# Attention and gated feed-forward on one core: a new order of scores and value products in the second half of the first batch

## The chip, the core and the metric

The kernel runs on one core of one Trainium2 chip. The metric is device time in microseconds for one launch, lower is better. A core has TensorE (matrix products, which write into PSUM), VectorE, ScalarE and GpSimd (elementwise work), and SyncE, which here only issues DMAs. GpSimd issues DMAs too. Each engine works through its own queue of instructions in order and waits at an instruction until the semaphores that it names have arrived. PSUM has eight banks of 128 x 512 fp32 here.

## The reference

Two steps follow each other, on 4 batches of 768 tokens with 8 heads of 64.

First an attention in which a query sees the first 8 keys (the globals) and the last 96 keys up to itself, with a bias that falls with the distance:

```
scores = q @ k.T / sqrt(64) - slope[h] * dist        # dist = 96 for globals out of the window
scores = where(is_global | is_local, scores, -1e9)
attn   = softmax(scores) @ v                          # (4, 8, 768, 64)
```

Then, with the heads of a token side by side as x (3072 x 512), a gated feed-forward:

```
out = (maximum(x @ w_gate, 0) * (x @ w_val)) @ w_out  # w_gate, w_val: 512 x 1536; w_out: 1536 x 512
```

## The kernel before, in words

**Tiling.** The work is cut into eight halves of 384 tokens, two to a batch; a half is called s in the attention and chunk c in the feed-forward. Heads go in pairs p = 0 to 3. Keys are cut into seven tiles j of 120 keys with the 8 globals in front of each. Chunk c needs the attention of half s = c, of all four pairs, as the bf16 tile xT.

**Attention of the first two halves (s = 0, 1).** For a pair p the pieces are:

- C(p), `piece_cast` (line 240): the fp32 q and k of the pair are cast to bf16, two instructions, on an engine chosen by s and p. In half 1 before the change: pair 0 GpSimd, 1 ScalarE, 2 VectorE, 3 GpSimd.
- T(p), `piece_t`: TensorE transposes them into one av bank, and four VectorE copies bring them to qT and kT.
- BI(p, g) and SC(p, g): the keys' tiles are in two groups g. The bias of a group is written into a score tile of two PSUM banks, the scores are added to it, and ScalarE's Exp (line 356) makes the bf16 tile es. Two such score tiles are in turn in half 1.
- AW(p), `piece_av_wide` (line 417): ten products with a matrix of ones give the softmax sums, ten with v the values (line 431). ScalarE takes Ln of the sums (line 437) and Exp of its negative (line 439), and VectorE multiplies the values with it into xT (line 442). Sums and values are two tiles of the av pool (two banks), except in half 0 for odd p, where they are the two banks of one score tile.

**Feed-forward.** `ffn_pieces` (line 477) gives for each of 12 blocks fc a gate tile (line 485, four products, then a relu on ScalarE, line 488) and a value tile (line 495, four products, then VectorE's multiply with the relu, line 497), and then the output products (line 504). Until the end of half 1 gate and value tiles share two PSUM banks; later they have three.

**Order.** It is written out by hand: pieces are called one after the other, and each engine's queue has its instructions in the order of these calls. `attention_pieces` (line 445) returns the list of a half; for half 1 its argument `fill` has six feed-forward pieces of chunk 0 which stand between the attention's pieces: value tiles 2 and 3, gate tiles 4, 5 and 6, value tile 4. Ahead of the list gates 0 to 3 and value tiles 0 and 1 are called, after it value tiles 5 and 6, gate 7, value tile 7; then chunk 1 begins. Which bank of a pool a tile gets is decided when the program is built: the one that is planned to be free first. So two tiles that are taken one after the other can lie in one bank.

**GpSimd's queue.** After half 0's list it holds the cast of pair 0 of half 1 (`piece_cast(1, 0)`), the loads of v for half 1, and the loads of weight group 1 (`load_w_group(1)`: gate and value weights of blocks 4 to 7, lines 168 to 176), then casts from half 1's list, then group 2 and the memsets that let SyncE's loads of q and k of half 2 begin.

Of the kernel before, what the change touches and what calls it, by code (L numbers as in the profile page):

```python
# [10 lines left out]
AF = mybir.ActivationFunctionType  # L11
# [4 lines left out]
def kernel(  # L16
# [12 lines left out]
    nc = tc.nc  # L29
# [9 lines left out]
    QH = S // 2  # L39
# [6 lines left out]
    scale = 1.0 / math.sqrt(D)  # L46
# [63 lines left out]
    GW = 4  # L110
# [29 lines left out]
    def load_v_globals(b):  # L140
        nc.gpsimd.dma_start(out=v_dst(b, 0, NG, 0),
                            in_=v[b, :, 0:NG, :].rearrange("h p d -> p h d"))

    def spread_v_globals(b, j0=1, j1=NT):
        for j in range(j0, j1):
            nc.sync.dma_start(out=v_dst(b, 0, NG, j), in_=v_dst(b, 0, NG, 0))
# [16 lines left out]
    def load_v_half(s):  # L163
        b, half = divmod(s, 2)
        if half == 0 and s > 2:
            load_v_globals(b)
            spread_v_globals(b)
        for j in range(4) if half == 0 else range(4, NT):
            load_v(b, j)

    def load_w(dst, src, f0, f1):
        nc.gpsimd.dma_start(out=dst, in_=src[:, f0:f1].rearrange("(c p) f -> p c f", p=128))

    def load_w_group(i):
        load_w(wg[i], moe_w_gate, i * GW * 128, (i + 1) * GW * 128)
        load_w(wv[i], moe_w_val, i * GW * 128, (i + 1) * GW * 128)
# [64 lines left out]
    def piece_cast(s, p):  # L241
        qk = cast_pool.tile([128, 2, NN, 2, D], BF16, name="qk")
        cast_of[s, p] = qk
        for i, src in ((1, ks_of[s]), (0, qs_of[s])):
            copy = nc.gpsimd.tensor_copy
            if s == 0:
                copy = (nc.vector.tensor_copy, nc.scalar.copy, nc.scalar.copy, nc.vector.tensor_copy)[p]
            elif s == 1 and p in (1, 2):
                copy = (nc.scalar.copy, nc.vector.tensor_copy)[p - 1]
            copy(  # L250
                qk[:, i].rearrange("t n e d -> t e n d"),
                src[:, 2 * p : 2 * p + 2, :].rearrange("t e (n d) -> t e n d", n=NN))
# [164 lines left out]
    def piece_av_wide(s, p):  # L417

        todo = [t for group in first_groups[s] for t in group]
        if s == 0 and p % 2 == 1:  # L420
            t = P["qk"].tile([128, 2, 512], FP32, name="qk_ps")
            av = [t[:, i] for i in range(2)]
        else:
            av = [av_psum.tile([128, 512], FP32, name="av_ps") for _ in range(2)]
        for what in range(2):
            av3 = av[what][:, 0:QH].rearrange("d (n p) -> d n p", n=NN)
            for i, (j, a, w, m) in enumerate(todo):
                es, c = es_of[s, p, j]
                for e in range(2):
                    z0 = D + 2 * D * (2 * p + e)  # L430
                    nc.tensor.matmul(av3[64 * e : 64 * e + 64, :, a : a + w],  # L431
                                     lhsT=ones if what == 0 else vbuf[0][:, j, z0 : z0 + D],
                                     rhs=es[:, e, c : c + NN * w].rearrange("k (n p) -> k n p", n=NN),
                                     start=(i == 0), stop=(i == len(todo) - 1),
                                     skip_group_check=True)
        ln = rc_pool.tile([128, QH], FP32, name="lnd")
        nc.scalar.activation(ln, av[0][:, 0:QH], AF.Ln, bias=0.0, scale=1.0)
        rc = rc_pool.tile([128, QH], FP32, name="rcp")
        nc.scalar.activation(rc, ln, AF.Exp, bias=0.0, scale=-1.0)
        if s not in xT_of:  # L440
            xT_of[s] = xt_pool.tile([128, N_DC, QH], BF16, name="xT")
        nc.vector.tensor_tensor(xT_of[s][:, p, :], av[1][:, 0:QH], rc, op=ALU.mult)

    def attention_pieces(s, fill=()):
        T = lambda p: [(0.34, lambda: piece_t(s, p))]
        QK = lambda p: [(0.18, lambda g=g: piece_qk(s, p, g)) for g in range(3)]
        AW = lambda p: [(0.58, lambda: piece_av_wide(s, p))]
        C = lambda p: [(0.0, lambda: piece_cast(s, p))]
        BI = lambda p, *gs: [(0.2, lambda g=g: piece_bias(s, p, g)) for g in gs]
        SC = lambda p, *gs: [(0.2, lambda g=g: piece_score(s, p, g)) for g in gs]  # L450
        X = lambda *fs: [(0.0, f) for f in fs]
        if s == 0:
            return (C(0) + X(lambda: load_v_globals(0), lambda: load_v(0, 0), lambda: load_v(0, 1),
                             lambda: load_v(0, 2), lambda: load_v(0, 3), lambda: load_w_group(0))
                    + C(1) + T(0) + BI(0, 0, 1) + C(2) + T(1) + SC(0, 0, 1) + BI(1, 0) + SC(1, 0) + C(3) + T(2)
                    + BI(1, 1) + SC(1, 1) + BI(2, 0) + T(3) + X(lambda: copy_v_globals(0, 1, 4))
                    + SC(2, 0) + BI(2, 1) + SC(2, 1)
                    + BI(3, 0) + SC(3, 0) + BI(3, 1) + SC(3, 1)
                    + AW(0) + AW(1) + X(lambda: load_qk_after(1, nc.vector, True)) + AW(2)
                    + AW(3) + X(second_pools, lambda: warm(4)))  # L460
        if s == 1:
            f = [[x] for x in fill]
            return (C(1) + T(0) + BI(0, 0, 1) + T(1) + C(2) + SC(0, 0, 1) + f[0] + BI(1, 0) + SC(1, 0)
                    + BI(1, 1) + SC(1, 1) + C(3) + T(2) + f[1] + BI(2, 0) + SC(2, 0) + BI(2, 1) + T(3)
                    + AW(0) + SC(2, 1) + BI(3, 0) + SC(3, 0) + f[2] + AW(1)
                    + BI(3, 1) + SC(3, 1) + f[3] + AW(2) + f[4] + f[5] + AW(3))
        AV = lambda p: [(0.29, lambda e=e: piece_av(s, p, e)) for e in range(2)]
        g = QK(3)
        a = AV(2)
        return (QK(0) + QK(1) + AV(0) + QK(2) + AV(1) + g[0:1] + a[0:1] + g[1:2] + a[1:2] + g[2:3]  # L470
                + [(0.0, lambda: None)] * 2 + AV(3))
# [2 lines left out]

    out_v = out.rearrange("(s p n) d -> s n p d", p=128, n=NN)

    def ffn_pieces(c):
        ht = ht_pool.tile([128, N_FC, QH], BF16, name="ht")
        st = {}

        def gate(fc):
            xT = xT_of[c]
            psg = P["ff"].tile([128, 512], FP32, name="ff_ps")
            for dc in range(N_DC):
                nc.tensor.matmul(psg[:, 0:QH], lhsT=w_of(wg, dc, fc), rhs=xT[:, dc, :],  # L485
                                 start=(dc == 0), stop=(dc == N_DC - 1))
            gr = gr_pool.tile([128, QH], BF16, name="grelu")
            nc.scalar.activation(gr, psg[:, 0:QH], AF.Relu, bias=0.0, scale=1.0)  # L488
            st[fc] = gr

        def val(fc):
            xT = xT_of[c]
            psv = P["ff"].tile([128, 512], FP32, name="ff_ps")
            for dc in range(N_DC):
                nc.tensor.matmul(psv[:, 0:QH], lhsT=w_of(wv, dc, fc), rhs=xT[:, dc, :],  # L495
                                 start=(dc == 0), stop=(dc == N_DC - 1))
            nc.vector.tensor_tensor(ht[:, fc, :], psv[:, 0:QH], st[fc], op=ALU.mult)  # L497

        def outp(n, part):
            if part == 0:  # L500
                st["o"] = P["ff"].tile([128, 512], FP32, name="ff_ps")
            ps2 = st["o"]
            for fc in range(part * N_FC // 2, (part + 1) * N_FC // 2):
                nc.tensor.matmul(ps2, lhsT=ht[:, fc, n * 128 : (n + 1) * 128],  # L504
                                 rhs=wo_sb[:, fc, :],
                                 start=(fc == 0), stop=(fc == N_FC - 1))
            if part == 1:
                osb = osb_pool.tile([128, DM], FP32, name="osb")
                nc.scalar.copy(osb, ps2)  # L509
                nc.sync.dma_start(out=out_v[c, n], in_=osb)  # L510

        f1 = []
        for fc in range(N_FC):
            f1.append((0.65, lambda fc=fc: gate(fc)))
            f1.append((0.65, lambda fc=fc: val(fc)))
        f2 = []
        for n in range(NN):
            for part in range(2):
                f2.append((1.3, lambda n=n, part=part: outp(n, part)))
        return f1, f2  # L520
# [26 lines left out]
        nc.gpsimd.memset(kT[0][p][:, 6, NG + 48 : 128].bitcast(mybir.dt.uint32), 0)  # L547
    piece_cast(1, 0)
    load_v_half(1)
    load_w_group(1)  # L550

    f1_0, f2_0 = ffn_pieces(0)
    f1_1, f2_1 = ffn_pieces(1)
    G = [slice(2 * GW * i, 2 * GW * (i + 1)) for i in range(N_FC // GW)]
    for i in (0, 2, 4, 6, 1, 3):
# [19 lines left out]
    for p in range(HP):  # L575
        piece_cast(2, p)
# [59 lines left out]
```

## Time and profile before

| | |
|---|---|
| median of 4 runs | 254.96 us (253.32 to 255.2) |
| the profiled execution's own time | 253.32 us |
| its span in the profile | 251.2 us |
| TensorE busy in the span | 241.0 us (96%) |
| ScalarE, VectorE, GpSimd busy | 158.3, 132.5, 88.6 us |
| granted TensorE clock, mean | 0.998 |

The profile is of one execution. "Busy" is the time in which an engine had an instruction at work; TensorE's products overlap, so the length of one row and the distance to the next row's start differ, and distances between starts are what adds up. In a row of the order in time the first number is the start in microseconds from the start of the span, the second the length of the merged group, and brackets hold the idle time ahead of it and what ended that. In a row of a stretch each engine has its busy time and its count.

### The profile page before, as it was taken

The numbers are of one execution on the slowest core, as the hardware profiler recorded it, in microseconds if no ns is written. First come the engines' busy times: TensorE is split into PE (matmuls) and PEld (weight loads), VectorE is DVE, ScalarE is ACT, GpSimd is POOL, SyncE is SP. The second block draws the span as 40 slices with busy tenths as digits, with TensorE's granted clock in tenths as the row PEclk, the third lists the DMA queues.
The fourth block names the chain that finished last, engine by engine and source line by source line (L and its number), as shares of the span: only waits on it lengthen the run. The fifth ranks groups of instructions, "written<-read, shape, count | busy, mean of one in ns | idle before, by whom it ended". The sixth has DMA issues, their size and how long they took to land.

```text
span 251.2 us, 4902 instructions
## 1 busy us (share of the span) xinstructions
PE 241.0 (96%) x1751; PEld 142.6 (57%) x1751; DVE 132.5 (53%) x338; ACT 158.3 (63%) x319; POOL 88.6 (35%) x211
## 2 busy tenths in 40 slices
PE   7789999999999999999999999999999999999993
PEld 3556665666555666556655666556555666556541
DVE  4745634875464657427662567437662557424410
ACT  5886785637675787557774787557774687553321
POOL 7907995500557327503626075303610000000000
PEclk9999999999999999999999999999999999999999
DMA  6999999981899995938469958838432100030012
GB/s 174 161 191 255 160 229 239 190 134 49 251 139 258 179 214 129 121 108 248 109 83 92 271 145 147 76 102 247 109 83 83 43 3 1 16 112 0 0 42 83
DMA packets 77559, 33.13 MB, mean 132 GB/s; under 512 B 53472, under 2 KB 74464, under 8 KB 77536
## 3 DMA queue, kind: packets, MB, share of 16 engines
q1 hardware_dynamic: 45680, 24.93, 37.2%
q0 software_dynamic: 31856, 7.91, 32.2%
q8 instruction: 13, 0.21, 0.4%
q14 instruction: 10, 0.08, 0.1%
HBM read 28.38 MB, written 6.29 MB: 138 GB/s over the span
## 4 chain that ended last, share of the span: by engine, by line
PE 82%; DVE 4%; ACT 4%; POOL 3%; DMA 3%; issue 1%; POOLq 0%; ACTq 0%; DVEq 0%
PE ff_ps L504 25%; PE ff_ps L485 22%; PE ff_ps L495 22%; PE av_ps L397 5%; PE qk_ps L369 4%; DMA wg<-in_moe_w_gate_dram 3%; DVE xT L414 2%; DVE ht L497 2%; POOL vbuf L155 1%; PE av_ps L281 1%; PE qk_ps L334 1%; PE av_ps L431 1%; ACT rcp L411 1%; ACT lnd L406 1%; ACT grelu L488 1%
## 5 line engine op out<-in xcount | busy, mean ns | idle before, releaser
L495 PE MATMUL ff_ps<-xT,wv 128*128 128x384 bf16 x384 | 77.8, 326 | 1.2 <-DVE ht L497 0.7
L485 PE MATMUL ff_ps<-xT,wg 128*128 128x384 bf16 x384 | 77.9, 326 | 0.6 <-DVE ht L497 0.5
L488 ACT ACTIVATE grelu<-ff_ps 128x384 bf16<-128x384 f32 x96 | 47.0, 489 | 33.1 <-PE ff_ps L485 16.9
L504 PE MATMUL ff_ps<-wo_sb,ht 128*128 128x512 bf16 x288 | 67.1, 379 | 0.0
L497 DVE TENSOR_TENSOR ht<-ff_ps,grelu 128x384 bf16<-128x384 f32 x96 | 53.4, 558 | 24.5 <-PE ff_ps L495 20.4
L414 DVE TENSOR_TENSOR xT<-av_ps,rcp 64x384 bf16<-64x384 f32 x48 | 26.6, 555 | 45.6 <-ACT rcp L411 42.7
L485 PEld LDWEIGHTS <-wg 128*128 128x128 bf16 x384 | 36.1, 97 | 24.5 <-issue 1.2
L495 PEld LDWEIGHTS <-wv 128*128 128x128 bf16 x384 | 36.1, 97 | 23.6 <-issue 2.7
L381 DVE TENSOR_TENSOR es<-es,m_all 128x432 bf16<-128x432 bf16 (+5 forms) x108 | 33.2, 335 | 22.4 <-ACT es L372 21.9
L372 ACT ACTIVATE es<-qk_ps 128x432 bf16<-128x432 f32 (+2 forms) x72 | 37.8, 528 | 10.3 <-PE qk_ps L369 8.4
L504 PEld LDWEIGHTS <-ht 128*128 128x128 bf16 x288 | 27.0, 97 | 28.2
L294 POOL CAST kc<-ks 128x384 bf16<-128x384 f32 x20 | 9.8, 533 | 59.1 <-DMA ks<-in_k_dram 59.1
L406 ACT ACTIVATE lnd<-av_ps 64x384 f32<-64x384 f32 x48 | 23.3, 485 | 11.7 <-PE av_ps L397 11.0
L509 ACT COPY osb<-ff_ps 128x512 f32<-128x512 f32 x24 | 14.0, 585 | 25.4 <-PE ff_ps L504 24.6
L369 PE MATMUL qk_ps<-qT,kT 128*128 128x432 bf16 (+5 forms) x108 | 24.8, 286 | 0.0
L155 POOL DMA_DIRECT2D vbuf<-in_v_dram x28 | 24.3, 878 | 0.6 <-issue 0.6
L397 PEld LDWEIGHTS <-vbuf 128*128 128x128 bf16 x216 | 18.0, 98 | 7.4
L397 PE MATMUL av_ps<-es,vbuf 128*128 128x216 bf16 (+4 forms) x216 | 21.0, 226 | 0.0
L369 PEld LDWEIGHTS <-kT 128*128 128x128 bf16 x108 | 10.6, 98 | 7.6
L302 POOL CAST qz<-qs 128x192 bf16<-128x192 f32 x40 | 12.6, 362 | 3.6 <-DMA qs<-in_q_dram 3.1
L411 ACT ACTIVATE rcp<-lnd 128x384 f32<-128x384 f32 x24 | 12.5, 522 | 0.8
L356 ACT ACTIVATE es<-qk_ps 128x864 bf16<-128x864 f32 (+3 forms) x16 | 10.6, 707 | 3.3 <-PE qk_ps L351 3.2
(77 smaller groups left out, 143.4 us busy)
## 6 DMA issues: line engine op xcount, KB each, us to landing
out_dram<-osb SPq DMA_DIRECT2D x24, 256.0 KB
ks<-in_k_dram SPq DMA_DIRECT2D x5, 768.0 KB
qs<-in_q_dram SPq DMA_DIRECT2D x5, 768.0 KB
vbuf<-in_v_dram POOLq DMA_DIRECT2D x24, 120.0 KB, 4.7
ks<-in_k_dram SPq DMA_DIRECT2D x12, 192.0 KB
qs<-in_q_dram SPq DMA_DIRECT2D x12, 192.0 KB
wg<-in_moe_w_gate_dram POOLq DMA_DIRECT2D x3, 512.0 KB, 7.7
wv<-in_moe_w_val_dram POOLq DMA_DIRECT2D x3, 512.0 KB, 9.5
```

Of the source, the lines that this page charges most:

```text
L155: nc.gpsimd.dma_start(out=v_dst(b, NG + r0, NG + r0 + n, j), in_=v[b, :, KT * j + r0 : KT * j + r0 + n, :].rearrange("h p d -> p h d"))
L369: nc.tensor.matmul(ps[:, c : c + n_], lhsT=kt[:, j, :], rhs=qd[:, :, :, a : a + w], start=True, stop=True)
L372: nc.scalar.activation(es[:, 0:cols], ps[:, 0:cols], AF.Exp, bias=0.0, scale=scale)
L381: nc.vector.tensor_mul(e4, e4, mk)
L397: nc.tensor.matmul(av3[:, :, a : a + w], lhsT=vb[:, j, z0 : z0 + 128], rhs=es[:, c : c + NN * w].rearrange("k (n p) -> k n p", n=NN), star ...
L406: nc.scalar.activation(ln[o0 : o0 + 64], av[d0 : d0 + 64, 0:QH], AF.Ln, bias=0.0, scale=1.0)
L414: nc.vector.tensor_tensor(xT_of[s][r, p, :], av_of[s, p, e_][r, 0:QH], rc[r], op=ALU.mult)
L485: nc.tensor.matmul(psg[:, 0:QH], lhsT=w_of(wg, dc, fc), rhs=xT[:, dc, :], start=(dc == 0), stop=(dc == N_DC - 1))
L488: nc.scalar.activation(gr, psg[:, 0:QH], AF.Relu, bias=0.0, scale=1.0)
L495: nc.tensor.matmul(psv[:, 0:QH], lhsT=w_of(wv, dc, fc), rhs=xT[:, dc, :], start=(dc == 0), stop=(dc == N_DC - 1))
L497: nc.vector.tensor_tensor(ht[:, fc, :], psv[:, 0:QH], st[fc], op=ALU.mult)
L504: nc.tensor.matmul(ps2, lhsT=ht[:, fc, n * 128 : (n + 1) * 128], rhs=wo_sb[:, fc, :], start=(fc == 0), stop=(fc == N_FC - 1))
```

## The change

Four things change, all of them in half 1 and chunk 0:

- the order of half 1's list: all bias and score pieces come ahead of the four value products; the fill pieces stand at other places, and pair 3's cast and transpose come earlier;
- value products of odd p take their two tiles from the score pool in half 1 too, as in half 0;
- the relus of gates 4, 5 and 6 of chunk 0 are VectorE instructions;
- of half 1's casts, pair 3 is VectorE's and pair 2 GpSimd's, and the latter is called ahead of the loads of weight group 1.

```diff
@@ piece_cast
-            elif s == 1 and p in (1, 2):
-                copy = (nc.scalar.copy, nc.vector.tensor_copy)[p - 1]
+            elif s == 1 and p % 2 == 1:
+                copy = (nc.scalar.copy, nc.vector.tensor_copy)[p // 2]
@@ piece_av_wide
-        if s == 0 and p % 2 == 1:
+        if p % 2 == 1:
@@ attention_pieces
-            return (C(1) + T(0) + BI(0, 0, 1) + T(1) + C(2) + SC(0, 0, 1) + f[0] + BI(1, 0) + SC(1, 0)
-                    + BI(1, 1) + SC(1, 1) + C(3) + T(2) + f[1] + BI(2, 0) + SC(2, 0) + BI(2, 1) + T(3)
-                    + AW(0) + SC(2, 1) + BI(3, 0) + SC(3, 0) + f[2] + AW(1)
-                    + BI(3, 1) + SC(3, 1) + f[3] + AW(2) + f[4] + f[5] + AW(3))
+            return (C(1) + T(0) + BI(0, 0, 1) + T(1) + SC(0, 0, 1) + f[0] + C(3) + BI(1, 0) + SC(1, 0)
+                    + BI(1, 1) + SC(1, 1) + T(2) + f[1] + BI(2, 0) + SC(2, 0) + T(3) + BI(2, 1) + SC(2, 1)
+                    + BI(3, 0) + SC(3, 0) + BI(3, 1) + SC(3, 1) + AW(0) + AW(1) + f[2] + AW(2) + f[3]
+                    + AW(3) + f[4] + f[5])
@@ ffn_pieces
-    def ffn_pieces(c):
+    def ffn_pieces(c, by_vector=()):
...
-            nc.scalar.activation(gr, psg[:, 0:QH], AF.Relu, bias=0.0, scale=1.0)
+            if fc in by_vector:
+                nc.vector.tensor_scalar_max(gr, psg[:, 0:QH], 0.0)
+            else:
+                nc.scalar.activation(gr, psg[:, 0:QH], AF.Relu, bias=0.0, scale=1.0)
@@ after half 0
     piece_cast(1, 0)
     load_v_half(1)
+    piece_cast(1, 2)
     load_w_group(1)
-    f1_0, f2_0 = ffn_pieces(0)
+    f1_0, f2_0 = ffn_pieces(0, range(GW, 2 * GW - 1))
```

## The prediction

> **What bounds the kernel now.** I read the stretches first, cut where the kernel's stages change, then TensorE's own waits in the stretch that the diff touches, then TensorE in order of time there.
>
> Stretches (the columns are busy time and count of TensorE, its weight loads, VectorE, ScalarE, GpSimd, then granted clock, DMA share, GB/s):
>
> ```profile
> 0.00:17.40 17.40, 13.49 (x163) 8.21 (x163) 8.92 (x33) 13.31 (x29) 10.84 (x25) 1.00 1.13 169
> 17.40:40.00 22.60, 21.46 (x250) 14.04 (x251) 12.19 (x31) 14.48 (x27) 18.48 (x40) 1.00 1.20 218
> 40.00:240.00 200.00, 198.81 (x1308) 117.29 (x1307) 111.28 (x274) 128.77 (x261) 59.27 (x147) 1.00 0.63 122
> ```
>
> From 40 us to the end TensorE is 99.4% busy at full clock, in an order that the diff doesn't change. So a microsecond won or lost before 40 us arrives at the end one for one, and nothing else counts. The change works between 17.4 and 40 us, where TensorE idles for 22.60 - 21.46 = 1.14 us. That is already close to the ceiling of any gain: 0.45% of the time.
>
> TensorE's waits from 17 to 40 us, then its order there (start, length, what, and in brackets the idle time and its releaser):
>
> ```profile
> PE av_ps L431 <- ACT lnd L437: 0.6, 1, 0.6
> PE ff_ps L485 <- DVE ht L497: 0.5, 1, 0.5
> PE ff_ps L485 <- DMA wg<-in_moe_w_gate_dram: 0.2, 1, 0.2
> ```
>
> ```profile
> 24.57 0.51 PE L334 MATMUL qk_ps<-dd,sid 128*128 128x216 bf16 x4
> ...
> 28.31 0.49 PE L431 MATMUL av_ps<-es,ones 128*64 128x216 bf16 x10
> 29.39 0.49 PE L431 MATMUL av_ps<-es,vbuf 128*64 128x216 bf16 x10 [0.58 <-ACT lnd L437]
> ...
> 35.76 0.49 PE L431 MATMUL av_ps<-es,ones 128*64 128x216 bf16 x10
> 36.10 0.47 PE L431 MATMUL av_ps<-es,vbuf 128*64 128x216 bf16 x10
> 36.50 1.48 PE L495 MATMUL ff_ps<-xT,wv 128*128 128x384 bf16 x8
> 38.45 0.81 PE L485 MATMUL ff_ps<-xT,wg 128*128 128x384 bf16 x4 [0.47 <-DVE ht L497]
> ```
>
> Two stalls. At 28.31 the first value product (pair 0) puts its sums into an av bank; its value half waits until ScalarE's Ln has read those sums, because the pool gave both tiles the same bank. At 38.45 gate 7 waits for a feed-forward bank that VectorE frees late, since the last xT multiply (37.38) stands ahead of it in VectorE's queue.
>
> **A sum to compare with.** From the starts in that order I take, per piece: transpose 0.34, first bias group 0.45, its scores 0.28, second bias group 0.36, its scores 0.23, one gate or value tile 0.65 (26.23 to 26.88), a whole value product 0.74 (33.62 to 34.36). From 24.57 (first bias of pair 1) to the first gate of chunk 1 stand: bias and scores of three pairs 3 x 1.32 = 3.96, two transposes 0.68, four value products 2.96, nine feed-forward tiles 5.85, together 13.45. A piece followed by a value product takes 0.1 longer (0.75 instead of 0.65 at 30.78, 32.87, 35.02; 0.43 instead of 0.34 at 27.88): four times, 0.40. Idle, start to start: 29.39 - 28.31 - 0.33 = 0.75, and 38.45 - 36.50 - 1.30 = 0.65. Sum 24.57 + 13.45 + 0.40 + 1.40 = 39.82; the trace has that gate at 39.75. So the sum is good to 0.1 us.
>
> **The change, part by part.**
>
> *Pools and order.* All products keep their number and shape, so 13.45 stays. With scores ahead, pair 0's product comes after pair 3's scores. In the built program its sums and values then lie in two av banks, pairs 1 and 3 use the score banks, pair 2 the av banks again. The 0.75 goes. Value products are entered after another kind of piece three times instead of four: 0.30, so -0.10. What is late next: the score groups now run without value products between them, and two score tiles go round. Pair 3's first bias needs the bank of pair 2's first scores. On my clock those scores start at 27.33, their Exp at 27.72 (as in the trace) and it lasts 0.85, to 28.57; TensorE reaches the bias at 28.54 (27.61 + transpose 0.34 + 0.36 + 0.23) and starts at 28.62, as the trace starts a bias 0.05 after the Exp it waits for. Cost 0.08. Pair 3's scores need the copies of its transpose, done on VectorE near 29.1, when they begin: nothing. Pair 2's product (32.3) needs pair 0's Ln and xT: ScalarE does the eight Exps to 30.87, then Ln, Exp of pair 0 to 31.8, xT to 32.4; the sums half hides it. If ScalarE were 0.3 us later, that would show.
>
> *Casts.* Pair 3's cast goes to VectorE, pair 2's to GpSimd. VectorE first has value tile 2's multiply (24.56 to 25.03), then the casts at the trace's spacing (0.75 each) to 26.53, so pair 2's transpose copies start 0.10 later than at 26.43; the scores that need the third copy have 0.10 to spare: nothing. Pair 2 on GpSimd is ready at 25.1 where its transpose starts at 25.89. The price is in GpSimd's queue:
>
> ```profile
> 23.48 0.65 POOL L155 DMA_DIRECT2D vbuf<-in_v_dram  x1
> 24.11 0.79 POOL L172 DMA_DIRECT2D wg<-in_moe_w_gate_dram  x1
> 24.88 0.77 POOL L172 DMA_DIRECT2D wv<-in_moe_w_val_dram  x1
> 25.62 0.56 POOL L250 CAST qk<-ks 128x384 bf16<-128x384 f32 x1
> 26.13 0.49 POOL L250 CAST qk<-qs 128x384 bf16<-128x384 f32 x1
> 26.58 0.75 POOL L172 DMA_DIRECT2D wg<-in_moe_w_gate_dram  x1
> ```
>
> The two casts move ahead of the loads of weight group 1: issue at 25.07 instead of 24.11; what follows them (group 2 at 26.58, then the memsets that release SyncE's q and k loads) keeps its time. Group 1's gate weights landed 6.5 us after issue, at 30.6, and gate 4 ran at 30.78: no slack in the old order. In the new one gate 4 stands behind two value products: scores end at 29.95, +0.10, + 2 x 0.74 = 31.53. A full shift gives 31.57, a wait of 0.04. I expect less: the packets under 512 B, which are those of v, run until 27.75 on the same queue, past the new issue's end (25.9), so the slowest DMA engines reach the weights no later. Bounds of the landing: 30.6 to 31.6; I take no wait. The value weights of group 1 (8.9 us, at most 34.8) meet value tile 4 at 35.1: hidden by 0.3.
>
> Here a rule speaks against the change. The Trainium skill, "SBUF — State Buffer", § Who interferes with whom, says that a VectorE copy or cast in its two-port modes and GpSimd take one port pair in turns and the second is blocked for the whole instruction, descriptor writing included. The new VectorE casts (25.03 to 26.6) lie upon the issue of group 1. But so do the old ones:
>
> ```profile
> 24.25 0.84 DVE L250 CAST qk<-ks 128x384 bf16<-128x384 f32 x1
> 25.00 0.82 DVE L250 CAST qk<-qs 128x384 bf16<-128x384 f32 x1
> ```
>
> Early in the kernel such a cast takes 0.36; here it is VectorE that loses, and the issue beside it takes 0.79 against 0.75 for group 2, beside which VectorE casts nothing. By the rule, with GpSimd the loser, two casts of 0.36 to 0.42 add up to 0.8 to the issue: landing 32.4 at worst, gate 4 waits 0.9, and the end is 255.3. By the row it is 0.04. I take the row.
>
> *Relus on VectorE.* Relus 4 to 6 leave ScalarE (0.49 each), which waits for nothing of importance by then. The trace has no VectorE relu; bounds for 384 columns out of PSUM are 0.35 (bf16 copy) and 0.56 (the multiply, fp32), and I take the multiply's row, next start after 0.47, since its PSUM input is fp32. Their place matters more: VectorE's queue becomes xT0, xT1, relu 4, xT2, relu 5, xT3, relu 6, then the multiplies. Let pair 3's product start at x. Today xT3 starts at x + 1.62 and the next VectorE instruction at x + 2.09. In the new order that is relu 6, done at x + 2.6; value tile 5 needs its bank, is wanted at x + 0.74 + 2 x 0.65 = x + 2.04 and starts at x + 2.65: a wait of 0.61. So the second stall isn't removed, it moves to another tile with nearly the same length. Gate 7 then needs the bank of value tile 5: a bank is free 1.53 after its tile starts (39.10 to 40.63, a tile that VectorE empties), two tiles take 1.30: 0.23 more. If the relu takes 0.35, both terms together are 0.7 instead of 0.84.
>
> **Sum.** 24.57 + 13.45 + 0.30 + 0.08 + 0.61 + 0.23 = 39.24 against 39.75 seen and 39.82 by the same sum: a gain of 0.5 to 0.6, say 0.55. The profiled execution would go from a span of 251.2 to 250.65. Its own time was 253.32, which is 2.1 more than the span, for start and end, untouched; it was the lowest of four runs with a median of 254.96. I take the same gain off the median: **254.4 us**.
>
> **Rivals.** (a) *Both stalls go*: VectorE's relu is at its short end and ScalarE's Ln and Exp of pair 3 come earlier, as ScalarE has no relus between. Then 1.3 us at most is won, 253.7. For it: TensorE's idle time in the stretch. Against it: xT3 is reached through ScalarE's fixed 0.54 + 0.52 + 0.56 behind pair 3's own sums, in both orders. (b) *Nothing is won*: the stretch of scores becomes bound by ScalarE's eight Exps with no slack (each wait 0.1 to 0.2, three of them), which gives the 0.55 back: 254.9. For it: Exp takes 0.85 and 0.63 a pair, 1.4 of the 1.32 + 0.34 that TensorE takes; against it: the two feed-forward tiles between. (c) *The gate weights are late*: gate 4 stands in TensorE's order ahead of everything that follows, and the loads of group 1 meet SyncE's q and k loads, issued from 28.21. If they land as slowly as the load behind them today (8.9 us), that is at 33.97 and gate 4 waits 2.4: 256.8. It decides from a landing at 32.1 (31.53 + 0.55) and costs over 0.5% from 33.4. For it: a load issued later in this queue took longer each time (6.5, 8.9, 11.4). Against it: what these wait for is the bytes ahead, and ahead of the gate weights stands the same v as before.
>
> **How the numbers follow.** Main case 0.58 (254.4, its own range 254.0 to 255.0); (a) 0.14; (b) 0.14; (c) 0.14. About 0.5%, 1.3 us, is what a measurement of this kernel can tell from no change; its four runs spread over 0.7%. Faster by more needs (a) in full, or a run median that falls low: 0.18. Slower by more needs most of (c): 0.18. Within 0.5%: 0.64. The range leaves out the far half of (c) and takes in (a) and the spread of medians: 253.3 to 255.8.
>
> **What would show it.** TensorE's idle 0.58 behind Ln at pair 0's values gone; a new idle of about 0.5 at value tile 5 (the value line), released by the VectorE relu, and 0.1 to 0.2 at gate 7; VectorE relus of 0.45 to 0.56; gate 4 near 31.5 with no wait for the weights; first gate of chunk 1 near 39.2; from there everything earlier by the same 0.5. Wrong if gate 4 waits for its DMA, if score groups wait for Exps by more than 0.1 each, or if the stretch after 40 us changes its length.

## The result: a small gain, of the size forecast, by a road that was partly another

The changed kernel takes 254.24 us in the median of 43 runs, against 255.07 us for the kernel before in 64 runs taken beside it; the ratio is 0.9975, with a 95% interval of 0.9961 to 0.999. That is 0.64 us less (0.25 to 1.0), where 0.55 was forecast. (The two medians are 0.83 apart; the ratio on record, over the fast runs, is not that of the medians, and ratios are compared below unless medians are named.) It lies within the 0.5% that the forecast called no change.

The profiled execution of the changed kernel took 254.73 us, with a span of 252.2 us. That is 1.0 us more than the span profiled before, although the medians go the other way; so the two profiles can't be subtracted as a whole, and are compared stage by stage. The stretches (same columns as before the change):

```profile
0.00:17.40 17.40, 13.88 (x166) 8.79 (x167) 9.00 (x34) 13.35 (x29) 10.86 (x25) 1.00 1.12 177
17.40:40.00 22.60, 19.86 (x243) 13.20 (x242) 12.97 (x34) 12.50 (x22) 18.52 (x40) 1.00 1.18 211
40.00:240.00 200.00, 198.99 (x1309) 117.35 (x1308) 110.95 (x274) 129.10 (x262) 59.65 (x147) 1.00 0.64 122
```

In the stretch from 17.40 to 40 us TensorE is busy for 1.6 us less than it was, that is, it waits more. Its waits from 17 to 45 us, and its order in time there:

```profile
PE ff_ps L485 <- DMA wg<-in_moe_w_gate_dram: 1.5, 1, 1.5
PE ff_ps L498 <- DVE grelu L489: 0.8, 1, 0.8
PE ff_ps L485 <- DVE xT L442: 0.3, 1, 0.3
```

```profile
25.74 0.51 PE L281 MATMUL av_ps<-ident,qk 128*128 128x128 bf16 x6
...
29.79 0.49 PE L431 MATMUL av_ps<-es,ones 128*64 128x216 bf16 x10
30.12 0.47 PE L431 MATMUL av_ps<-es,vbuf 128*64 128x216 bf16 x10
30.44 0.47 PE L431 MATMUL qk_ps<-es,ones 128*64 128x216 bf16 x10
30.75 0.47 PE L431 MATMUL qk_ps<-es,vbuf 128*64 128x216 bf16 x10
32.73 0.82 PE L485 MATMUL ff_ps<-xT,wg 128*128 128x384 bf16 x4 [1.50 <-DMA wg<-in_moe_w_gate_dram]
...
36.37 0.81 PE L498 MATMUL ff_ps<-xT,wv 128*128 128x384 bf16 x4
37.99 1.46 PE L498 MATMUL ff_ps<-xT,wv 128*128 128x384 bf16 x8 [0.81 <-DVE grelu L489]
39.45 0.81 PE L485 MATMUL ff_ps<-xT,wg 128*128 128x384 bf16 x4
40.10 0.81 PE L498 MATMUL ff_ps<-xT,wv 128*128 128x384 bf16 x4
40.75 0.81 PE L485 MATMUL ff_ps<-xT,wg 128*128 128x384 bf16 x4
```

The values of pair 0 follow their sums without a gap (29.79, 30.12): the stall of 0.75 is gone. The second stall moved to value tile 5 (37.99), released by a VectorE relu, as the forecast had it, but it is longer. And gate 4 (32.73) waits 1.5 us for its weights, which the forecast had at none. What the forecast had not looked at is in GpSimd's and VectorE's rows near 47 us, to which the experiments led.

A yardstick that leaves early differences out is the stage from the third transpose of half 1 (25.74 here) to chunk 1's first gate (40.75). It is 15.01 us here, and without gate 4's wait of 1.50 it is 13.51. In the kernel before it is 39.75 - 25.89 = 13.86. All runs in one table, in us; "rest" is the stage without gate 4's idle time, "landing" is from the issue of group 1's gate weights:

| profile | stage | gate 4 idle | rest | landing |
|---|---|---|---|---|
| before | 13.86 | 0 | 13.86 | 6.5 |
| changed | 15.01 | 1.50 | 13.51 | 8.1 |
| e1 (before, group 0) | 13.87 | 0 | 13.87 | 7.3 |
| e5 (before, memsets moved) | 15.58 | 1.65 | 13.93 | 8.3 |
| e9 (before, both) | 13.87 | 0 | 13.87 | 8.1 |
| e2 (changed, group 0) | 13.50 | 0 | 13.50 | 8.6 |
| e3 (changed, casts as before) | 13.70 | 0.20 | 13.50 | 7.4 |
| e6 (changed, memsets moved) | 13.72 | 0.22 | 13.50 | 7.3 |
| e7 (e6, cast between the loads) | 14.07 | 0.57 | 13.50 | 8.4 |
| e10 (changed, group 0, memsets moved) | 13.50 | 0 | 13.50 | 5.8 |
| e4 (changed, relus on ScalarE) | 12.92 | 0 | 12.92 | 6.2 |
| e8 (e7, relus on ScalarE) | 12.91 | 0 | 12.91 | 7.2 |
| e11 (e4, memsets moved) | 12.91 | 0 | 12.91 | 6.8 |

The "rest" hardly varies, 0.07 us among profiles of the same order. So the order's own gain in this stage is 0.36 us. What varies from one execution to the next is when the stage begins (25.68 to 27.06 us in these profiles), the landing of the weights, and what happens after the stage.

### The profile page after: what moved, and what is told of

It reads as the page before. It is cut to its first block, busy times and chain, and to the rows that moved or that the text cites. A ratio compares the mean times of both kernels' runs of the same rounds, so it can differ in the third digit from the quotient of the medians.

```text
span 252.2 us, 4907 instructions
## 1 busy us (share of the span) xinstructions
PE 241.0 (96%) x1751; PEld 142.9 (57%) x1751; DVE 133.5 (53%) x341; ACT 157.0 (62%) x316; POOL 89.0 (35%) x211
## 4 chain that ended last, share of the span: by engine, by line
PE 76%; DMA 6%; DVE 6%; ACT 6%; issue 2%; POOL 1%; SPq 1%; ACTq 0%; DVEq 0%
PE ff_ps L507 25%; PE ff_ps L498 20%; PE ff_ps L485 20%; PE av_ps L397 5%; PE qk_ps L369 4%; DMA wg<-in_moe_w_gate_dram 3%; DMA qs<-in_q_dram 3%; DVE ht L500 3%; DVE xT L414 2%; ACT grelu L491 1%; ACT rcp L411 1%; ACT lnd L406 1%; ACT es L356 1%; PE av_ps L281 1%; POOL vbuf L155 1%
## 5 line engine op out<-in xcount | busy, mean ns | idle before, releaser
L491 ACT ACTIVATE grelu<-ff_ps 128x384 bf16<-128x384 f32 x93 | 45.5, 489 | 34.5 <-PE ff_ps L485 18.6
L372 ACT ACTIVATE es<-qk_ps 128x432 bf16<-128x432 f32 (+2 forms) x72 | 37.9, 528 | 10.1 <-PE qk_ps L369 8.2
L356 ACT ACTIVATE es<-qk_ps 128x864 bf16<-128x864 f32 (+3 forms) x16 | 10.5, 708 | 3.4 <-PE qk_ps L351 3.3
## 6 DMA issues: line engine op xcount, KB each, us to landing
wv<-in_moe_w_val_dram POOLq DMA_DIRECT2D x3, 512.0 KB, 10.9
```

Of the source, the lines that this page charges most:

```text
L372: nc.scalar.activation(es[:, 0:cols], ps[:, 0:cols], AF.Exp, bias=0.0, scale=scale)
```

## The experiments

### Is gate 4's wait usual, and in which kernel? (e1, e2, e3, e4)

The theory at this point was the forecast's: the order wins about 0.55, and group 1's weights are just in time. The rival was that both kernels usually wait for them, and the profile before was of an execution that didn't.

e1 and e2 take the weights of another group in chunk 0, in the kernel before and in the changed one:

```diff
-lhsT=w_of(wg, dc, fc), rhs=xT[:, dc, :]
+lhsT=w_of(wg, dc, fc % GW if c == 0 and fc < 2 * GW else fc), rhs=xT[:, dc, :]
```

and the same for wv.

> The kernel before, with the gates and values 4 to 7 of chunk 0 computed from weight group 0 (long there) instead of group 1: these four blocks' results are not the reference's; instructions and their order stay. It shows what the kernel before usually pays for the landing of group 1. Theory of the prediction (group 1 lands just in time, gate 4 waits for nothing): same time as before, ratio 0.998 to 1.002. Rival (the profiled execution of before was a lucky one, and group 1 usually lands 1 to 2 us after gate 4's turn, as it did in the profile after): faster by 1 to 2 us, ratio 0.992 to 0.996.

Measured: 254.97 us, ratio 1.0007 (0.998 to 1.0035). No gain.

> The changed kernel, with the gates and values 4 to 7 of chunk 0 computed from weight group 0 (their results are not the reference's). Theory of the prediction: no wait for group 1 in most executions, so the same time as the changed kernel, ratio to before 0.997 to 0.998. Rival (the 1.5 us wait at gate 4 in the profile after is usual): 1.5 us less than the changed kernel, ratio to before 0.991 to 0.993, and the whole first gate of chunk 1 comes near 39.2 us in its profile.

Measured: 254.23 us, ratio 0.9986 (0.9967 to 1.0004). No gain over the changed kernel, though its stage took 13.50 and gate 4 waited for nothing. TensorE's only waits between 17.6 and 52 us, in its order:

```profile
19.28 2.36 PE L485 MATMUL ff_ps<-xT,wg 128*128 128x384 bf16 x13 [0.34 <-DVE xT L442]
37.81 1.46 PE L498 MATMUL ff_ps<-xT,wv 128*128 128x384 bf16 x8 [0.81 <-DVE grelu L489]
50.78 0.81 PE L485 MATMUL ff_ps<-xT,wg 128*128 128x384 bf16 x4 [1.36 <-DVE ht L500]
```

There is a new stall of 1.36 us at 50.78, after the stretch that the change touches; neither of the first two profiles had one of this length.

e3 undoes the casts' part alone:

```diff
-    piece_cast(1, 2)
     load_w_group(1)
...
-elif s == 1 and p % 2 == 1:  # pair 1 ScalarE, pair 3 VectorE
+elif s == 1 and p in (1, 2): # pair 1 ScalarE, pair 2 VectorE
...
-T(1) + SC(0, 0, 1) + f[0] + C(3)
+T(1) + C(2) + SC(0, 0, 1) + f[0] + C(3)
```

> The changed kernel with the casts as in the kernel before: pair 2 on VectorE, called ahead of pair 0's scores, pair 3 on GpSimd behind the loads of group 1, whose issue is then 1.0 us earlier. If the landing of group 1 follows its issue and gate 4 waits for it: 1.0 us faster than the changed kernel, ratio to before 0.993 to 0.994. If the landing is set by the v packets ahead, or gate 4 doesn't wait: as the changed kernel, 0.997 to 0.998.

Measured: 254.86 us, ratio 1.0011 (0.9982 to 1.0039). This meets neither expectation: it is not faster than the changed kernel, if anything slower, though the intervals overlap. Its profile has the same stall behind the stage, 1.47 us at 50.65.

e4 undoes the relus' part alone (`ffn_pieces(0)` instead of `ffn_pieces(0, range(GW, 2 * GW - 1))`).

> The changed kernel with all relus on ScalarE. By the prediction's step the wait of value tile 5 (0.6 forecast, 0.81 idle in the profile after) comes from relu 6 standing behind the last xT multiply in VectorE's queue; on ScalarE relu 6 follows the Exp of pair 3 directly and is done 0.5 us earlier. Expected: 0.4 to 0.5 us faster than the changed kernel, ratio to before 0.995 to 0.996. Rival (the relus on VectorE are what made the change faster): slower than the changed kernel, 0.999 to 1.001.

Measured: 254.46 us, ratio 0.9975 (0.9956 to 0.9993). The stage is 0.59 us shorter, where 0.4 to 0.5 was expected, and TensorE has no wait on record between 17.6 and 49 us; but the time is that of the changed kernel. Half 2's first transpose starts at 44.17, against 45.18 in the profile before, and then:

```profile
46.45 0.50 PE L281 MATMUL av_ps<-ident,qk 128*128 128x128 bf16 x6
46.79 0.81 PE L498 MATMUL ff_ps<-xT,wv 128*128 128x384 bf16 x4
49.07 0.81 PE L485 MATMUL ff_ps<-xT,wg 128*128 128x384 bf16 x4 [1.47 <-DVE ht L500]
```

VectorE and GpSimd in the same moment (e4, in order of time):

```profile
46.09 0.17 DVE L266 COPY kT<-av_ps 128x24 bf16<-128x24 bf16 x1
46.21 2.78 DVE L267 COPY kT<-kT 128x56 bf16<-128x56 bf16 x1
46.27 2.69 POOL L583 MEMSET qz<- 128x1536 uint32 x2
```

This is the row that matters. VectorE's small copy of the globals, from SBUF to SBUF, takes 0.18 us when it is alone. Here it takes 2.78 us and ends with GpSimd's two memsets, 46.21 + 2.78 = 48.99 against 46.27 + 2.69 = 48.96. Everything behind it in VectorE's queue waits, the multiply that frees a bank for TensorE among it. The Trainium skill, "SBUF — State Buffer", § Who interferes with whom, has the rule: a VectorE copy in a two-port mode and a GpSimd instruction take one port pair in turns, and the one that loses waits for the whole instruction. That this copy runs in such a mode no run shows; that it lasts until the memsets end, the rows do. In the profile before the same copy meets the memsets later in their course and waits less:

```profile
45.55 2.69 POOL L579 MEMSET qz<- 128x1536 uint32 x2
...
47.22 1.05 DVE L267 COPY kT<-kT 128x56 bf16<-128x56 bf16 x1
```

There VectorE is free again at 48.27 and TensorE waits for nothing. In the profile after the copy starts 1.32 us behind the memsets' start, and TensorE loses 0.25 (a gate at 49.70 instead of 49.45):

```profile
46.90 2.69 POOL L583 MEMSET qz<- 128x1536 uint32 x2
...
48.22 1.41 DVE L267 COPY kT<-kT 128x56 bf16<-128x56 bf16 x1
```

The memsets' start follows the landing of half 2's q and k, since they stand behind the casts of these in GpSimd's queue; the copy's follows TensorE. Once the memsets are under way, the earlier TensorE comes, the more of them is still ahead of the copy. So a gain in the stage is given back at a second place.

How usual gate 4's wait is, e1 and e2 don't settle. Their times show no 1.5 us taken away, but in both profiles TensorE lost something at the copy (1.36 in e2; 0.23 in e1, where the copy took 1.39). The profiles say a little more. Ten of the fourteen use group 1's own weights, and gate 4 waits in six of them; in the old order it waits in two of three (e5, e12).

### Taking the collision away (e5 to e8)

New theory: the copy's collision with the memsets eats gains of the stage. The memsets move to where GpSimd waits for q and k:

```diff
-    for p in range(HP):
-        piece_cast(2, p)
-    spread_v_globals(1)
+    piece_cast(2, 0)
     for i in range(2):
         nc.gpsimd.memset(qz[1 - i]...)
+    for p in range(1, HP):
+        piece_cast(2, p)
+    spread_v_globals(1)
```

> The kernel before with one thing moved: GpSimd's two memsets of qz (2.69 us together, line 579, at 45.55 in its profile) are called right behind the cast of pair 0 of half 2, where GpSimd waits for q and k anyway, instead of behind the cast of pair 3. Theory now (VectorE's copy of the globals from kT to kT, line 267, takes 0.18 us alone and 1.05 to 2.79 us when GpSimd's memset is under way; where it meets the memset's start, TensorE loses 1.4 us near 50 us): the copy is back at 0.18 in the profile, and the time falls by 0 to 1 us, ratio 0.996 to 0.999. Rival (VectorE's wait is hidden in the kernel before): 0.999 to 1.001.

Measured: 255.37 us, ratio 1.0017 (0.9996 to 1.0038). The copy is at 0.18 us, and the time doesn't fall. So the rival holds: in the kernel before VectorE's wait costs nothing that can be measured. Its profile brought something else, on TensorE, in the order of the kernel before:

```profile
30.23 0.49 PE L431 MATMUL av_ps<-es,vbuf 128*64 128x216 bf16 x10 [0.58 <-ACT lnd L437]
33.35 0.82 PE L485 MATMUL ff_ps<-xT,wg 128*128 128x384 bf16 x4 [1.65 <-DMA wg<-in_moe_w_gate_dram]
41.02 0.81 PE L485 MATMUL ff_ps<-xT,wg 128*128 128x384 bf16 x4 [0.48 <-DVE ht L497]
```

So gate 4 waits for its weights in the old order too; the profile before was of an execution in which they landed early.

> The changed kernel with the memsets of qz moved in the same way. Theory (the change brings TensorE to half 2's transposes earlier, so that the copy meets the start of the memset more often, and part of the gain is given back there): more is won than by the same move in the kernel before, ratio to before 0.991 to 0.995. Rival (the collision has no part in the result): ratio 0.997 to 0.998, as the changed kernel.

Measured: 253.77 us, ratio 0.9953 (0.9932 to 0.9974), just above the range expected, which its interval takes in for the most part. It overlaps that of the changed kernel, so this alone doesn't decide on the collision. Against e5, which has the same move in the old order, the intervals are disjoint: 0.9953 / 1.0017 is 1.6 us. Of this the stage's order is 0.36; in the two profiles gate 4 waits 1.65 us in the old order and 0.22 in the new one, which would more than make up the rest. One profile of each doesn't show that all their runs waited so.

e7 also calls the cast of pair 2 between the loads of the gate and the value weights:

```diff
-    piece_cast(1, 2)
-    load_w_group(1)
+    load_w(wg[1], moe_w_gate, GW * 128, 2 * GW * 128)
+    piece_cast(1, 2)
+    load_w(wv[1], moe_w_val, GW * 128, 2 * GW * 128)
```

> The changed kernel with the memsets of qz moved, and the cast of pair 2 on GpSimd called between the loads of the gate and the value weights of group 1 instead of ahead of both: the gate weights are issued 1.0 us earlier. If gate 4's wait follows the issue: 0.5 to 1.0 us less than with the memsets moved alone, ratio 0.988 to 0.993. If the landing is set by the v packets ahead: the same as with the memsets moved alone.

Measured: 254.03 us, ratio 0.9959 (0.9938 to 0.998): no gain by the earlier issue, and in its profile gate 4 waits 0.57 all the same.

> As the run before it in this list, with all relus on ScalarE besides. In the run with only the relus on ScalarE TensorE had no wait at value tile 5 (0.81 idle in the profile after) but lost 1.47 us at 49 us to the collision. With the collision gone, 0.6 to 0.8 us less than the same kernel with three relus on VectorE: ratio 0.985 to 0.991. Rival (ScalarE's relus delay its Ln and Exp, so that the wait comes back elsewhere): no less.

Measured: 253.42 us, ratio 0.9943 (0.992 to 0.9967). The stage has its 0.59 us less; in the time 0.6 us less than e7 in the medians, within what the intervals allow, short of the range that was expected against before.

### Both disturbances away, and the parts (e9 to e12)

e9 and e10 combine the edits of e1 and e5 in the kernel before, of e2 and e6 in the changed one.

> The kernel before with both disturbances taken away: gates and values 4 to 7 of chunk 0 from weight group 0 (their results are not the reference's), and the memsets of qz moved behind the cast of pair 0. If gate 4 usually waits for group 1 in the kernel before (1.65 us idle in the profile with the memsets moved), and what removing it won was given back at the collision (that removal alone gave 1.0007): 0.5 to 1.5 us faster than before, ratio 0.994 to 0.998. If gate 4's wait is rare in the kernel before: 0.999 to 1.002, as with the memsets moved alone.

Measured: 254.31 us, ratio 0.9984 (0.9959 to 1.0009). The interval takes in much of both expectations and decides neither.

> The changed kernel with both disturbances taken away (the same four blocks' results are not the reference's). In the profiles so far the stage from the third transpose of half 1 to chunk 1's first gate takes 13.86 us in the kernel before and 13.50 in the changed one when gate 4 waits for nothing. So 0.36 us less than the run before it in this list, ratio between the two 0.9986; against before 0.992 to 0.996. Rival (the change's gain is not the order, but that it hides group 1's landing): no less than the run before it.

Measured: 253.71 us, ratio 0.9947 (0.9919 to 0.9974). That the change gains only by hiding the landing is ruled out in the profiles: the stages are 13.87 and 13.50, with gate 4 waiting for nothing in both, so the order gains 0.37 by itself. That it hides the landing besides is not ruled out. The times, 0.9947 / 0.9984 = 0.9963, say rather more than 0.37, but with intervals of 0.25% on each they can't tell 0.36 us from 0.9. The mean spans of the runs (252.3 us in e9, 251.3 in e10) are 1.0 apart. By an estimate from the mean granted clocks of the runs, 0.9969 and 0.9981, the clock is 0.3 of that. Whether the order gains something outside the stage stays open.

> The changed kernel with the memsets of qz moved and all relus on ScalarE, the cast of pair 2 staying ahead of both loads. The stage should take 12.9 us instead of 13.5 (12.92 in the run with the relus alone). Expected: 0.5 to 0.6 us less than with the memsets moved alone (0.9953), ratio to before 0.992 to 0.994; the same as with the cast between the loads (0.9943) if that cast's place makes no difference, 0.3 or more slower than it if it does.

Measured: 253.51 us, ratio 0.9928 (0.9904 to 0.9952). Against e4, which differs in the memsets alone (0.9956 to 0.9993), the intervals are just disjoint, each against runs of the kernel before beside it: the collision cost that order 0.47%, 1.2 us. With e4's stall of 1.47 us this is shown from both sides. The other two pairs of the new order that differ in the memsets alone go the same way, with intervals that overlap: 0.9975 to 0.9953 from the changed kernel to e6, 0.9986 to 0.9947 from e2 to e10. TensorE and VectorE in e11, where e4 lost it:

```profile
47.83 0.81 PE L498 MATMUL ff_ps<-xT,wv 128*128 128x384 bf16 x4
48.48 0.81 PE L485 MATMUL ff_ps<-xT,wg 128*128 128x384 bf16 x4
```

```profile
47.25 0.18 DVE L267 COPY kT<-kT 128x56 bf16<-128x56 bf16 x1
49.41 0.18 DVE L267 COPY kT<-kT 128x56 bf16<-128x56 bf16 x1
```

e11 is also the best version found: the changed kernel's order and pools and casts, relus on ScalarE as before the change, memsets moved; it beats the kernel before by 0.5 to 1.0%, and by the ratios the changed one by half a per cent. It can't be told from e8.

e12 does the pools' part alone, in the kernel before (`if p % 2 == 1:` in `piece_av_wide`).

> The kernel before with only the pool part of the change: value products of odd pairs take both tiles from the score pool in half 1. Theory (the 0.75 stall is pair 0's, whose two tiles still lie in one av bank; an Ln on a shared two-bank tile waits for the values too, and the score banks are held longer): not faster, ratio 0.999 to 1.004. Rival (the pools alone bring the gain): 0.997 to 0.998.

Measured: 255.79 us, ratio 1.0028 (1.0007 to 1.0049): not faster, as expected, and slower by 0.7 us. Half of that may be the clock: its runs were granted 0.9964 in the mean, those of the kernel before beside them 0.9978, by estimate 0.35 us. Pair 0's stall stays, and gate 7's grows from 0.47 to 0.81:

```profile
29.99 0.49 PE L431 MATMUL av_ps<-es,vbuf 128*64 128x216 bf16 x10 [0.58 <-ACT lnd L437]
42.10 0.81 PE L485 MATMUL ff_ps<-xT,wg 128*128 128x384 bf16 x4 [0.81 <-DVE ht L497]
```

## Why the prediction was right, and where it wasn't

The two stalls did what was forecast, and the total came out in the range. But two of the prediction's own signs of being wrong came true as well: gate 4 waited for its DMA in the profile after, and in e2, e3 and e4 the stretch behind 40 us grew by a stall of about 1.4 us. That 0.55 and 0.64 lie so close is luck in part: in the stage the order gained 0.36 and not 0.51, gate 4's weights came late where no wait was forecast, and a collision behind the stage took gains back.

**The stall at pair 0 goes.** Right: 29.79 and 30.12 leave 0.33 between sums and values, against 1.08 before.

**Score groups ahead.** Right: TensorE's longest hold-up in them is 0.07 start to start (scores at 28.16, the next bias at 28.47, 0.31 instead of 0.24), where 0.08 was forecast; the casts of pairs 2 and 3 and their copies delay nothing. So rival (b) didn't come.

**The second stall moves to value tile 5.** Right in its place and its releaser, but mis-sized: from value tile 4 to value tile 5 it is 37.99 - 36.37 - 0.65 = 0.97 against 0.61 in the sum. The sum let pair 3's Ln start 0.54 after the product, as it does when sums and values are two tiles. In the score pool they are one tile of two banks, and the Ln waits for the values as well. Two rows of ScalarE show it, the last Ln before the change and after it:

```profile
36.30 0.49 ACT L437 ACTIVATE lnd<-av_ps 128x384 f32<-128x384 f32 x1 [0.59 <-PE av_ps L431]
```

```profile
35.84 0.49 ACT L437 ACTIVATE lnd<-qk_ps 128x384 f32<-128x384 f32 x1 [0.78 <-PE qk_ps L431]
```

Their products started at 35.76 and at 34.97, so the Ln came 0.54 and 0.87 later. These 0.33 are most of the difference; e12, with the pools alone, shows the same 0.34 at gate 7. The VectorE relu for which value tile 5 waits stands behind the last multiply, as forecast:

```profile
36.92 0.56 DVE L442 TENSOR_TENSOR xT<-qk_ps,rcp 128x384 bf16<-128x384 f32 x1 [0.80 <-ACT rcp L439]
37.39 0.55 DVE L489 TENSOR_SCALAR grelu<-ff_ps 128x384 bf16<-128x384 f32 x1
```

It lasts 0.55 to 0.56, with 0.46 to the next start (37.39 to 37.85), as taken. Gate 7 waits 0.16 (39.45 - 37.99 - 1.30), forecast 0.23. The three idle terms are 0.07 + 0.97 + 0.16 = 1.20 where 0.92 was counted, and the pieces took some 0.1 less than counted. So the order's gain becomes 0.36 where the sum had 39.75 - 39.24 = 0.51. Rival (a), both stalls gone, came with one part undone: e4, with the relus on ScalarE, has neither.

**Group 1's weights: no wait.** Wrong for the profiled execution. The weights landed 8.1 us after their issue, at 32.6:

```profile
24.53 0.79 POOL L172 DMA_DIRECT2D wg<-in_moe_w_gate_dram  x1
```

```profile
DMA to landing us min/median/max: 8.1/8.1/8.1
```

That is beyond the 32.1 from which rival (c) was to decide. The step treated the 6.5 us of one execution as what the load takes; over 14 profiles (e12's included, 7.9) it is 5.8 to 8.6. Its reason, that the load waits for the packets of v ahead of it, failed too. Packets under 512 B end near 27.75 in the profile before, by 27.25 in the profile after and by 26 in e7, and the weights land at 30.6, 32.6 and 31.7.

As far as so few profiles can tell, the later issue is only in part passed on. Counted from the first v load, the weights land 9.0 to 10.9 us later where they are issued 2.5 us behind it (eight profiles, mean 10.1), and 9.2 to 12.0 where they are issued 3.4 us behind it (six profiles, mean 10.5). What sets the landing is open; e7 won nothing by issuing earlier. That gate 4's turn comes later in the new order may hide more of the wait than before: in e5 the old order lost 1.65 there, and e6 beats e5 by 1.6. That this makes up the difference between 0.36 and the measured 0.64 is argued, not shown; the interval of the ratio holds 0.36 too.

**From 40 us on nothing changes, and a gain arrives one for one.** This step failed. It was read from TensorE's 99.4% there, in an execution in which VectorE's copy came late enough. e4 came 1.0 us earlier and lost 1.47 at 49.07. The forecast named no such rival. That the total came out right owes something to this: the relus on VectorE, which cost 0.59 in the stage, cost nothing in the time as long as the collision took it (e4, 0.9975, against the changed kernel, 0.9975).

**The casts and the port.** For the casts the row was the better guide: in the profile after, the issue of group 1 took 0.79 and 0.76 us beside VectorE's casts, that of group 2 0.75 and 0.76. But row and rule need not be opposed. By the rule as the prediction quotes it the second instruction is blocked, and in the profile before each cast begins behind an issue (24.25 behind 24.11, 25.00 behind 24.88) and is held. Where a cast begins ahead, the issue pays, though little. In e7 the casts at 24.88 and 25.18 take 0.38 and 0.35, and the issue at 24.95 takes 0.89; in e9 the casts at 25.16 and 25.50 take 0.41 and 0.34, and the issue at 25.28 takes 0.87. That is about 0.1 us more and not 0.8. The rule bore harder on another pair of instructions, the copy and the memsets, which the prediction had not looked at.

## What to carry to other kernels

An engine that is busy for 99% of a stage shows what that stage takes as things are timed now, not what it takes when work arrives earlier; look in the stages behind for pairs of instructions that are kept apart only by their times, above all SBUF copies on VectorE and long memsets on GpSimd. When two results are put into one tile, as in the score pool here, whoever reads the first waits for the second. And a single profile gives one draw of a DMA's landing: where work stands just behind a landing, ask for several profiles before calling it hidden.

## What the runs showed that was not expected

The VectorE copy loses to the memsets even when its row begins first: 46.21 against 46.27 in e4, where it lasts 2.78 us. The VectorE row ahead of it ends at 46.26, so from the start of the rows alone one can't tell which of the two was first at work. The two VectorE casts took 0.84 and 0.82 us in the profile before and 0.56 and 0.34 in the profile after, both times with GpSimd's issue of group 1 beside them. Not every cast that begins behind an issue is held: the last of these is not (25.43 behind 25.31), nor is the first in e4 (25.02 behind 24.95, 0.35 us long). Why is open.

The granted clock can fall for some microseconds. In e12, behind gate 4's wait of 1.20 us, the stretch from 32 to 38 us, in steps of two, has in its third last column 0.73, 0.50 and 0.92:

```profile
32.00:34.00 2.00, 1.35 (x8) 0.55 (x10) 0.00 (x0) 0.43 (x2) 2.00 (x7) 0.73 1.20 218
34.00:36.00 2.00, 2.00 (x32) 1.84 (x28) 0.00 (x0) 1.14 (x3) 2.00 (x3) 0.50 1.18 231
36.00:38.00 2.00, 2.00 (x32) 1.24 (x27) 0.56 (x1) 1.75 (x4) 2.00 (x3) 0.92 1.19 231
```

Taken against full clock that is by estimate 2 x (0.27 + 0.50 + 0.08) = 1.7 us, more than the whole effect of the change, and one reason why e12's stage isn't in the table. Gate 4's wait of 1.50 in the profile after was followed by no such dip (1.00 from 17.40 to 40 us).
